# One core, local attention into a feed-forward layer: each engine's order written as a schedule of slots, weights loaded through other queues

## The chip, the core and the metric

One core of a Trainium2 chip runs the kernel. It has five engines that work side by side, each through its own list of instructions in order: TensorE (matmuls, into the accumulation memory PSUM), VectorE, ScalarE, GpSimd, and SyncE, which here only issues transfers (DMAs). An instruction waits on semaphores for what it needs, and everything behind it on its engine waits with it. The profile calls the engines PE, DVE, ACT, POOL and SP; PEld is TensorE's weight load. The metric is device time in microseconds (us).

## The reference

Attention over 4 batches, 8 heads, 768 positions and 64 values per head. A query sees its last 96 keys and the first 8 keys of the sequence, with a bias that grows with distance. The result, as 3072 tokens of 512 values, goes through a feed-forward layer of width 1024 with a gate h * softmax(h) and a layer norm without mean shift.

```python
    scores = scale * np.matmul(q, k.transpose(0, 1, 3, 2))
    is_global = pos[None, :] < int(n_global)
    is_local = (rel >= 0) & (rel < int(n_local))
    ...
    bias = -slopes[:, None, None] * dist[None, :, :]
    scores = np.where(keep, scores + bias, -1e9)
    a = np.exp(scores - max); a = a / (sum(a) + 1e-09)
    x = np.matmul(a, v)
    ...
    h = x @ w_in
    solu = h * softmax(h)
    ln = (solu - mu) / np.sqrt(var + 1e-06) * g_ln
    return ln @ w_out
```

(Lines of the reference, shortened.)

## The kernel before

The work is cut into 12 units of 256 queries, three in each batch (s = 0, 1, 2), and each unit's feed-forward into two tiles of 128 tokens, r0 and r1. For a unit the steps are: q and k are loaded, cast to 16 bits by GpSimd (L211) and turned on TensorE by eight matmuls each against a unit matrix (L227); VectorE copies them out of PSUM as qT and kT (L234, L240). Four groups of heads have scores (L262), an Exp on ScalarE (L267) and a product with a mask of bias and window on VectorE (L269). The eight global keys have small matmuls of their own (gs, L281; Exp L287; values pv, L294). Sums of the weights (lp, L307 and L315) go through Ln and Exp on ScalarE to 1/l (rl, L322); four transfers spread rl over the partitions as rlb (L326). Values (pa, L343, L351) times rlb give xT on VectorE (L358).

The feed-forward of a tile: ph = xT w_in, eight matmuls with 512 columns (L370); Exp on ScalarE (e, L377); the product un on VectorE (L380); Square on ScalarE (L386); five GpSimd instructions on a column of 128 that give the norm's factor rs (L391 to L398). Then eight transposes of un (lT, L406), a copy by VectorE (uT, L408), eight matmuls with gw (po, L411), and the scaling by rs, on VectorE for r0 (L419), on ScalarE for r1 (L421), into osb, which SyncE stores (L423).

gw is w_out times g_ln, less its mean over the rows: scaled on VectorE, averaged by eight matmuls (gbar, L458), and centred on VectorE (L461). The masks are 16 Exps on ScalarE (L203) of distances that VectorE works out from GpSimd's indices. All transfers are issued by SyncE, in one queue. w_in comes as 32-bit numbers and is cast on VectorE.

PSUM has three buffers of two banks ("big": scores, ph, pa) and two of one bank ("small": turned q and k, gs, pv, lp, lT, po).

The order is written by a weave: while the feed-forward of unit i is issued step by step (ff_in of a tile, then ff_out of the tile before), the attention of unit i + 2 is issued between its steps, two units ahead. From this order the framework's scheduler makes each engine's list, by its own estimates of when things are ready; it moves single matmuls past each other.

Of the kernel before, what the change touches and what calls it, by code (L numbers as in the profile page):

```python
# [16 lines left out]
P = 128  # L17
# [5 lines left out]
def kernel(  # L23
# [86 lines left out]
    def constants():  # L110
        c = held
        c["ident"] = ident = const.tile([P, P], FP16, name="ident")
# [5 lines left out]

# [15 lines left out]
        far = msb.tile([P, W0 + W1], FP32, name="far", tag="osb", bufs=2)
# [37 lines left out]
        for g in range(NPAIR):  # L172
            for m in range(2):
                nc.gpsimd.tensor_copy(
                    out=selV[:, g, m * NG : m * NG + NG].rearrange("p (r i) -> p r i", r=2),
                    in_=ident.rearrange("p (r i) -> p r i", r=2)[:, :, 0 : NG // 2],
                )
# [21 lines left out]

    def masks(kind):  # L200
        o, w = ((0, W0), (W0, W1))[kind]
        for h in range(H):
            nc.scalar.activation(out=held["mask"][:, h // 2, h % 2, o : o + w],  # L203
                                 in_=held["dist"][:, o : o + w],
                                 func=AF.Exp, scale=-slopes[h])


    def cast_qk(b, s):
        for name in "qk":
            t = attn.tile([P, 2, H, D], FP16, name=name + "16")  # L210
            nc.gpsimd.tensor_copy(  # L211
                out=t, in_=held.pop((name + "32", b, s)).rearrange("p h (r d) -> p r h d", r=2)
            )
            held[name + "16", b, s] = t
# [7 lines left out]
    def turn(b, s, name):  # L222
        src = held.pop((name + "16", b, s))
        pt_ = small([P, NPAIR, 2, P], FP16, "p" + name)
# [7 lines left out]
        if name == "q":  # L232
            qT = attn.tile([P, NPAIR, 2, QC], FP16, name="qT")
            nc.vector.tensor_copy(out=qT, in_=pt_)  # L234
            held["qT", b, s] = qT
            return
        if s == 0:
# [4 lines left out]
            in_=pt_.rearrange("p g r (j i) -> p (g r) j i", j=2),  # L242
        )
        if s == 0:
            z = held["kgz"][b % 2]
            for m in range(2):
                rr = slice(m * D, m * D + D)
                nc.gpsimd.tensor_copy(
                    out=z[rr, :, m * NG : m * NG + NG].rearrange("p g (r i) -> p g r i", r=2),
                    in_=kT[rr, 0, :, :, 0 : NG // 2],  # L250
                )

    def scores(b, s, g):
# [13 lines left out]
        nc.scalar.activation(out=pt[:, :, 0:w], in_=sc[:, :, 0:w], func=AF.Exp, scale=inv_sqrt_d)  # L267
        o = W0 if s else 0
# [6 lines left out]
    def global_scores(b, s):  # L275
# [3 lines left out]
        gs = small([P, 2, n], FP32, "gs")  # L279
# [6 lines left out]
        pg = attn.tile([P, 2, n], FP16, name="pg", bufs=3)  # L286
        nc.scalar.activation(out=pg, in_=gs, func=AF.Exp, scale=inv_sqrt_d, bias=held["gb"])  # L287
        held["pg", b, s] = pg

    def global_values(b):  # L290
        pv = small([P, HD], FP32, "pv")
        v0 = attn.tile([P, HD], FP16, name="v0", bufs=1)
        nc.gpsimd.tensor_copy(out=v0.rearrange("p (h d) -> p h d", d=D), in_=held["v16", b][:, :, 0])
        nc.tensor.matmul(out=pv, lhsT=held["selV"].rearrange("p g c -> p (g c)"), rhs=v0,  # L294
# [6 lines left out]
    def sums(b, s):  # L301
        i0 = gstart(s)
        lp = small([P, 2, QC], FP32, "lp")
# [14 lines left out]
        )  # L318
        ln = attn.tile([P, UQ], FP32, name="ln")
        nc.scalar.activation(out=ln, in_=lp.rearrange("p r i -> p (r i)"), func=AF.Ln)  # L320
        rl = attn.tile([P, UQ], FP32, name="rl")
        nc.scalar.activation(out=rl, in_=ln, func=AF.Exp, scale=-1.0)  # L322
        rlb = attn.tile([P, NPAIR, UQ], FP32, name="rlb", bufs=3)
# [7 lines left out]
        held["rlb", b, s] = rlb  # L331

    def values(b, s, gs):
        if gs[0] == 0:
            held["po", b, s] = big("pa").rearrange("p a f -> p (a f)").rearrange(
                "p (g r i) -> p g r i", g=NPAIR, r=2)
        po = held["po", b, s]
        i0 = gstart(s)
        for g in gs:
# [10 lines left out]
        for g in gs:  # L350
# [5 lines left out]
    def norm(b, s):  # L356
        xT = attn.tile([P, NPAIR, UQ], FP16, name="xT", bufs=3)
        nc.vector.tensor_tensor(  # L358
            out=xT, in0=held.pop(("po", b, s)).rearrange("p g r i -> p g (r i)"),
# [5 lines left out]
    def ff_in(b, s, r):  # L365
        xT = held["xT", b, s]
        ph = big("ph").rearrange("p a f -> p (a f)")
        for j in range(NCC):
            for fh in range(2):
                nc.tensor.matmul(  # L370
                    out=ph[:, ds(fh * 512, 512)], lhsT=xT[:, j, ts(r, P)],
# [3 lines left out]
        e = msb.tile([P, D_FF], FP16, name="e")  # L375
        s0 = msb.tile([P, 1], FP32, name="s0", bufs=6)
        nc.scalar.activation(out=e, in_=ph, func=AF.Exp, accum_out=s0)  # L377
        un = msb.tile([P, D_FF], FP16, name="un", bufs=4)
        s1 = msb.tile([P, 1], FP32, name="s1", bufs=6)
        nc.vector.scalar_tensor_tensor(  # L380
            out=un, in0=e, scalar=1.0, in1=ph,
            op0=ALU.mult, op1=ALU.mult, accum_out=s1,
        )
        sq = msb.tile([P, D_FF], FP16, name="sq", bufs=1)
        s2 = msb.tile([P, 1], FP32, name="s2", bufs=6)
        nc.scalar.activation(out=sq, in_=un, func=AF.Square, accum_out=s2)  # L386
# [13 lines left out]
        held["un", b, s, r], held["rs", b, s, r] = un, rs  # L400

    def ff_out(b, s, r):
        un, rs = held.pop(("un", b, s, r)), held.pop(("rs", b, s, r))
        lT = small([P, NFC, P], FP16, "lT")
        for u in range(NFC):
            nc.tensor.transpose(out=lT[:, u, :], in_=un[:, ts(u, P)], identity=held["ident"])  # L406
        uT = msb.tile([P, NFC, P], FP16, name="uT")
        nc.vector.tensor_copy(out=uT, in_=lT)  # L408
        po = small([P, D_MODEL], FP32, "po")
        for u in range(NFC):  # L410
# [3 lines left out]
            )  # L414
        if r == 0:
# [6 lines left out]
        if r == 1:  # L422
            nc.sync.dma_start(  # L423
                out=out[ds(b * S + s * UQ, UQ), :].rearrange("(p r) c -> p (r c)", r=2),
                in_=osb.rearrange("p r c -> p (r c)"),
# [3 lines left out]
    def w32(name):  # L429
        return stage.tile([P, 2 * D_MODEL], FP32, name=name, tag="w32", bufs=4)  # L430
# [147 lines left out]
```

## Time and profile before

| | us |
|---|---|
| median of 3 runs | 225.37 (224.7 to 228.64) |
| the profiled execution, its own time | 224.81 |
| its span, first to last instruction | 223.1 |
| mean granted TensorE clock | 0.965 |
| TensorE, VectorE, ScalarE, GpSimd busy | 174.8, 134.5, 120.3, 96.8 |

All that follows is read from the one profiled execution. A busy matmul in it includes its drain, which overlaps with the next one, so TensorE's busy time is more than its work; what it must do is better read from the distance between the starts of two pieces.

### The profile page before, as it was taken

How to read it: one execution, taken by the hardware profiler on the slowest of the kernel's cores; microseconds unless marked ns; L12 is line 12 of the kernel's file. 1: busy time of each engine (PE TensorE's matmuls, PEld its weight loads, DVE VectorE, ACT ScalarE, POOL GpSimd, SP SyncE). 2: the span in 40 equal slices, each digit the busy share in tenths (PEclk: the TensorE clock that was granted, in tenths of full speed). 3: DMA queues.
4: the chain of work that ended last, by engine and by line, in shares of the span. 5: the costliest groups of instructions: out<-in, count | busy, mean ns of one | idle time of the engine just before them, and what ended most of it. 6: DMA issues, size and time to landing. Idle time of an engine off the chain costs nothing.

```text
span 223.1 us, 4309 instructions
## 1 busy us (share of the span) xinstructions
PE 174.8 (78%) x1656; PEld 91.5 (41%) x1656; DVE 134.5 (60%) x215; ACT 120.3 (54%) x209; POOL 96.8 (43%) x196
## 2 busy tenths in 40 slices
PE   0247884679779799889799888996995995999962
PEld 0123542335435435535455345453353453454430
DVE  6784486865664844838765575767348357448550
ACT  2296530095663647583674845846454845746641
POOL 8934303353299253159366224954431231223340
PEclk9999999699996979999999999999699999999998
DMA  6999998999933999570799964973051213223022
GB/s 167 268 359 201 274 330 218 247 161 230 248 132 81 254 160 165 132 249 7 194 304 212 183 140 111 268 209 79 0 165 26 95 25 72 93 46 133 16 94 94
DMA packets 61188, 35.93 MB, mean 161 GB/s; under 512 B 27376, under 2 KB 58096, under 8 KB 61168
## 3 DMA queue, kind: packets, MB, share of 16 engines
q1 hardware_dynamic: 61168, 35.66, 69.9%
q8 instruction: 13, 0.21, 0.4%
q14 instruction: 7, 0.06, 0.1%
HBM read 23.07 MB, written 6.29 MB: 132 GB/s over the span
## 4 chain that ended last, share of the span: by engine, by line
PE 23%; DVE 7%; issue 7%; ACT 6%; DMA 5%; SPq 3%; POOL 2%; POOLq 0%; DVEq 0%
PE ph L370 8%; PE po L411 8%; DMA rlb<-rl 5%; SPq L326 3%; DVE un L380 2%; ACT e L377 2%; DVE uT L408 2%; PE lp L307 2%; ACT osb L421 1%; PE pa L343 1%; DVE pt L269 1%; PE lT L406 1%; DVE kT L240 1%; POOL w L397 1%; DVE xT L358 1%
## 5 line engine op out<-in xcount | busy, mean ns | idle before, releaser
L370 PE MATMUL ph<-w_in,xT 128*128 128x512 f16 x192 | 52.5, 406 | 7.6 <-DVE xT L358 5.4
L411 PE MATMUL po<-gw,uT 128*128 128x512 f16 x192 | 47.4, 388 | 4.2 <-DVE uT L408 3.0
L377 ACT ACTIVATE e<-ph 128x1024 f16<-128x1024 f32 x24 | 24.6, 1023 | 44.4 <-PE ph L370 44.2
L267 ACT ACTIVATE pt<-sc 128x896 f16<-128x896 f32 (+1 forms) x48 | 40.1, 858 | 5.4 <-PE sc L262 5.2
L269 DVE TENSOR_TENSOR pt<-pt,mask 128x896 f16<-128x896 f16 (+1 forms) x48 | 31.1, 660 | 18.3 <-ACT pt L267 17.9
L380 DVE SCALAR_TENSOR_TENSOR un<-e,ph 128x1024 f16<-128x1024 f16 x24 | 29.2, 1218 | 10.2 <-ACT e L377 10.0
L386 ACT ACTIVATE sq<-un 128x1024 f16<-128x1024 f16 x24 | 25.4, 1057 | 15.4 <-DVE un L380 15.3
L262 PE MATMUL sc<-qT,kT 64*128 64x224 f16 (+2 forms) x256 | 18.5, 246 | 17.7 <-ACT pt L267 6.6
L411 PEld LDWEIGHTS <-uT 128*128 128x128 f16 x192 | 18.3, 101 | 27.5 <-DVE uT L408 8.2
L370 PEld LDWEIGHTS <-xT 128*128 128x128 f16 x192 | 17.7, 102 | 26.5 <-issue 5.7
L391 POOL TENSOR_SCALAR w<-s 128x1 f32<-128x1 f32 x24 | 6.3, 261 | 48.7 <-ACT e L377 48.7
L393 POOL TENSOR_SCALAR w<-s,w 128x1 f32<-128x1 f32 x24 | 12.7, 531 | 26.4 <-DVE un L380 26.3
L419 DVE TENSOR_SCALAR osb<-po,rs 128x512 f32<-128x512 f32 x12 | 9.0, 750 | 21.3 <-POOL rs L398 13.4
L211 POOL CAST q<-q 128x1024 f16<-128x1024 f32 x12 | 13.1, 1091 | 18.3 <-DMA q<-in_q_dram 8.0
L262 PEld LDWEIGHTS <-kT 64*128 64x128 f16 x256 | 9.2, 98 | 27.1 <-issue 15.6
L408 DVE COPY uT<-lT 128x1024 f16<-128x1024 f16 x24 | 16.5, 686 | 5.9 <-PE lT L406 5.9
L343 PE MATMUL pa<-pt,v 128*64 128x128 f16 (+2 forms) x256 | 17.1, 256 | 0.5 <-ACT pt L267 0.5
L358 DVE TENSOR_TENSOR xT<-pa,rlb 128x1024 f16<-128x1024 f32 x12 | 14.6, 1218 | 2.4 <-DMA rlb<-rl 2.3
L211 POOL CAST k<-k 128x1024 f16<-128x1024 f32 x12 | 14.0, 1168 | 3.9 <-DMA k<-in_k_dram 3.3
L421 ACT ACTIVATE osb<-po,rs 128x512 f32<-128x512 f32 x12 | 8.2, 684 | 13.8 <-issue 6.9
L227 PE MATMUL pq<-ident,q 128*128 128x128 f16 x96 | 8.5, 233 | 9.0 <-POOL q L211 9.0
L406 PE MATMUL lT<-ident,un 128*128 128x128 f16 x192 | 15.1, 223 | 0.0
(68 smaller groups left out, 212.6 us busy)
## 6 DMA issues: line engine op xcount, KB each, us to landing
q<-in_q_dram SPq DMA_DIRECT2D x12, 512.0 KB, 4.9
k<-in_k_dram SPq DMA_DIRECT2D x12, 512.0 KB, 6.3
rlb<-rl SPq DMA_DIRECT2D x48, 128.0 KB, 2.8
out_dram<-osb SPq DMA_DIRECT2D x12, 512.0 KB, 2.7
v<-in_v_dram SPq DMA_DIRECT2D x6, 768.0 KB, 10.5
w_in<-in_moe_w_in_dram SPq DMA_DIRECT2D x4, 512.0 KB, 6.0
w_out<-in_moe_w_out_dram SPq DMA_DIRECT2D x4, 512.0 KB, 6.6
v<-in_v_dram SPq DMA_DIRECT2D x12, 128.0 KB, 5.1
```

The source lines that it names most:

```text
L211: nc.gpsimd.tensor_copy(out=t, in_=held.pop((name + "32", b, s)).rearrange("p h (r d) -> p r h d", r=2))
L262: nc.tensor.matmul(out=sc[:, m, o : o + e - a].rearrange("p (r i) -> p r i", r=2), lhsT=kT[r, j, g].rearrange("p r i -> p (r i)"), rhs=qT[ ...
L267: nc.scalar.activation(out=pt[:, :, 0:w], in_=sc[:, :, 0:w], func=AF.Exp, scale=inv_sqrt_d)
L269: nc.vector.tensor_tensor(out=pt[:, :, 0:w], in0=pt[:, :, 0:w], in1=held["mask"][:, g, :, o : o + w], op=ALU.mult)
L343: nc.tensor.matmul(out=po[m * D : m * D + D, g, :, a // 2 : e // 2], lhsT=held["v16", b][:, 2 * g + m, j], rhs=pt[:, m, o : o + e - a].rea ...
L370: nc.tensor.matmul(out=ph[:, ds(fh * 512, 512)], lhsT=xT[:, j, ts(r, P)], rhs=held["w_in"][:, j, ds(fh * 512, 512)], start=(j == 0), stop= ...
L377: nc.scalar.activation(out=e, in_=ph, func=AF.Exp, accum_out=s0)
L380: nc.vector.scalar_tensor_tensor(out=un, in0=e, scalar=1.0, in1=ph, op0=ALU.mult, op1=ALU.mult, accum_out=s1,)
L386: nc.scalar.activation(out=sq, in_=un, func=AF.Square, accum_out=s2)
L406: nc.tensor.transpose(out=lT[:, u, :], in_=un[:, ts(u, P)], identity=held["ident"])
L408: nc.vector.tensor_copy(out=uT, in_=lT)
L411: nc.tensor.matmul(out=po, lhsT=uT[:, u, :], rhs=held["gw"][:, u, :], start=(u == 0), stop=(u == NFC - 1),)
```

## The change

The scheduler is switched off. Each step is cut into its engine's part (scores, expo, keep; sums, invert, spread; ff_in, ff_exp, ff_mul, ff_square, ff_stats, ff_turn, ff_evac, ff_out, ff_scale, store), and a plan gives each part a slot and a time in it. The parts are sorted by slot x 13.2 + time, and this order alone stands on every engine; the numbers set an order, not a time. Slot i holds the feed-forward in of unit i, the output of unit i - 1 (one slot behind its input), the attention of unit i + 1, the turning of q and k of unit i + 2 and the load of q and k of unit i + 3. Slots -2 and -1 are the start.

The rest: q and k are turned into one big buffer; loads of w_in are issued by GpSimd and cast on the way, w_out and g_ln are issued by ScalarE; w_out is scaled on GpSimd; distances and masks are worked out in two halves, the second after the softmax of unit 0; q of unit 0 is cast on ScalarE; rlb and xT have two buffers, not three, un five, not four; the last unit is stored in two halves.

```diff
     def turn(b, s, name):
+        if name == "q":
+            held["turned"] = psum.tile([P, 2, NPAIR, 2, P], FP16, name="qk", tag="big", bufs=3)
         src = held.pop((name + "16", b, s))
-        pt_ = small([P, NPAIR, 2, P], FP16, "p" + name)
+        pt_ = held["turned"][:, "qk".index(name)]
...
     def load_w_in():
         held["w_in"] = const.tile([P, NCC, D_FF], FP16, name="w_in")
-        held["w_in32"] = [w32(f"w_in32_{j}") for j in range(NCC)]
-        for j in range(NCC):
-            nc.sync.dma_start(out=held["w_in32"][j], in_=moe_w_in[ts(j, P), :])
-
-    def cast_w_in():
-        for j in range(NCC):
-            nc.vector.tensor_copy(held["w_in"][:, j, :], held["w_in32"][j])
+        wv = moe_w_in.rearrange("(j p) f -> p j f", p=P)
+        for j in range(0, NCC, 2):
+            nc.gpsimd.dma_start(out=held["w_in"][:, j : j + 2], in_=wv[:, j : j + 2])
...
-        held["w_out32"] = []
-        for j in range(0, NFC, 2):
-            t = w32(f"w_out32_{j}").rearrange("p (j c) -> p j c", j=2)
-            nc.sync.dma_start(out=t, in_=wv[:, j : j + 2])
-            held["w_out32"] += [t[:, 0], t[:, 1]]
...
+        t = stage.tile([P, NFC, D_MODEL], FP32, name="w_out32", bufs=1)
+        for j in range(0, NFC, 4):
+            nc.scalar.dma_start(out=t[:, j : j + 4], in_=wv[:, j : j + 4])
+        held["w_out32"] = [t[:, j] for j in range(NFC)]
+
+    def scale_w_out(j):
+        if j == 0:
+            held["gw"] = const.tile([P, NFC, D_MODEL], FP16, name="gw")
+        nc.gpsimd.tensor_scalar(
+            out=held["gw"][:, j, :], in0=held["w_out32"][j], scalar1=held["g32"][:, j : j + 1],
+            scalar2=0.0, op0=ALU.mult, op1=ALU.add,
+        )
...
+    T = 13.2
+    plan = []
+
+    def at(slot, t, f, *args):
+        plan.append((slot * T + t, len(plan), f, args))
...
+        at(i - 2, 10.7, turn, b, s, "q")
+        at(i - 2, 11.3, turn, b, s, "k")
+        at(i - 2, 11.35, evac_q, b, s)
+        at(i - 2, 12.0, evac_k, b, s)
...
+        times = ((0, 4.6, 6.4, 7.65, 9.85), (1, 8.96, 11.1, 12.7, T + 0.5))
...
-    for i in range(N):
-        loads(i + 4)
-        prep(i + 3)
-        weave(attention(i + 2) if i + 2 < N else [], feed(i))
-    ff_out(*tiles[-1])
+    with tc.manual_schedule():
+        for _, _, f, args in sorted(plan, key=lambda x: x[:2]):
+            f(*args)
```

What this does to the lists. VectorE in the middle of the program, before: the copies of uT and xT stand between mask products, at places that differ from unit to unit.

```order
L380 SCALAR_TENSOR_TENSOR un,s_1233<-e,ph 128x1024
L408 COPY uT<-lT 128x1024
L269 TENSOR_TENSOR pt<-pt,mask 128x896 x3
L408 COPY uT<-lT 128x1024
L380 SCALAR_TENSOR_TENSOR un,s_1330<-e,ph 128x1024
L269 TENSOR_TENSOR pt<-pt,mask 128x896
L358 TENSOR_TENSOR xT<-pa,rlb 128x1024
L419 TENSOR_SCALAR osb<-po,rs 128x512
L234 COPY qT<-pq 128x1024
L240 COPY kT<-pk 128x8x2x64
L380 SCALAR_TENSOR_TENSOR un,s_1476<-e,ph 128x1024
L408 COPY uT<-lT 128x1024
```

VectorE in the same part, after: one pattern in every slot, here from un of r1 to the next.

```order
L414 SCALAR_TENSOR_TENSOR un,s_1266<-e,ph 128x1024
L447 COPY uT<-lT 128x1024
L385 TENSOR_TENSOR xT<-pa,rlb 128x1024
L290 TENSOR_TENSOR pt<-pt,mask 128x896
L465 TENSOR_SCALAR osb<-po,rs 128x512
L290 TENSOR_TENSOR pt<-pt,mask 128x896
L447 COPY uT<-lT 128x1024
L290 TENSOR_TENSOR pt<-pt,mask 128x896 x2
L414 SCALAR_TENSOR_TENSOR un,s_1397<-e,ph 128x1024
L248 COPY qT<-qk 128x1024
L255 COPY kT<-qk 128x8x2x64
L414 SCALAR_TENSOR_TENSOR un,s_1512<-e,ph 128x1024
```

The un of r1 stands behind qT and kT and directly ahead of uT of r0; xT comes ahead of all mask products of its slot.

SyncE at the start, before (q, k, v: the inputs; w_in, g, w_out: weights; rlb: the spread of 1/l):

```order
L86 DMA q_155<-in_q_dram 128x8x128
L86 DMA k_157<-in_k_dram 128x8x128
L104 DMA v_75<-in_v_dram 64x8x64 x8
L444 DMA g_167<-in_moe_g_ln_dram 128x8x1
L449 DMA w_out_0_169<-in_moe_w_out_dram 128x2x512
L449 DMA w_out_2_171<-in_moe_w_out_dram 128x2x512
L449 DMA w_out_4_173<-in_moe_w_out_dram 128x2x512
L449 DMA w_out_6_175<-in_moe_w_out_dram 128x2x512
L86 DMA q_177<-in_q_dram 128x8x128
L86 DMA k_179<-in_k_dram 128x8x128
L326 DMA rlb<-rl 128x1x256 x8
```

SyncE at the start, after:

```order
L86 DMA q_82<-in_q_dram 128x8x128
L86 DMA k_84<-in_k_dram 128x8x128
L86 DMA q_86<-in_q_dram 128x8x128
L86 DMA k_88<-in_k_dram 128x8x128
L356 DMA rlb<-rl 128x1x256 x4
L104 DMA v_77<-in_v_dram 64x8x64 x8
L86 DMA q_351<-in_q_dram 128x8x128
L86 DMA k_353<-in_k_dram 128x8x128
L356 DMA rlb<-rl 128x1x256 x4
```

The weights have left this list, the rlb of unit 0 stands directly behind q and k of unit 2, and the second part of v behind it.

SyncE in a slot that loads v, after (osb is the stored output):

```order
L356 DMA rlb<-rl 128x1x256 x4
L86 DMA q_1277<-in_q_dram 128x8x128
L86 DMA k_1279<-in_k_dram 128x8x128
L98 DMA v_1286<-in_v_dram 64x48x64 x2
L473 DMA out_dram<-osb 128x1024
L356 DMA rlb<-rl 128x1x256 x4
L86 DMA q_1523<-in_q_dram 128x8x128
```

The store and the rlb of the slot stand behind the two loads of v, as they did before.

## Rows read from the trace of the kernel before

**Rows 1.** The cores view, then the page's line of busy engines: us, share, instructions.

```profile
core 0: 223.1 us, clock 0.965
...
PE 174.8 (78%) x1656; PEld 91.5 (41%) x1656; DVE 134.5 (60%) x215; ACT 120.3 (54%) x209; POOL 96.8 (43%) x196
```

**Rows 2.** Tile view of osb: duration ns min/median/max, first and last start us.

```profile
L421 ACT ACTIVATE osb<-po,rs x12: 668/687/689, 62.3 to 218.9; 128x512 f32<-128x512 f32 x12
```

**Rows 3.** The chain that ended last, two steady stretches: start us, us, what.

```profile
125.73 0.22 PE gs L281 x4
...
126.11 1.83 PE ph L370 x8
127.95 0.30 PE sc L262 x6
...
128.59 0.57 PE lT L406 x8
...
133.30 0.49 PE lp L307 x21
133.79 0.21 PE lp L315
...
134.65 0.45 PE pq L227 x8
...
197.25 1.73 PE po L411 x8
198.97 0.32 PE pa L343 x6
199.29 0.33 PE pa L351 x2
```

**Rows 4.** Timeline of one tile: start us, us, engine, line, what, [idle before].

```profile
200.30 1.02 ACT L377 ACTIVATE e<-ph 128x1024 f16<-128x1024 f32 x1 [2.18 <-PE ph L370]
...
201.44 1.22 DVE L380 SCALAR_TENSOR_TENSOR un<-e,ph 128x1024 f16<-128x1024 f16 x1
...
202.71 1.06 ACT L386 ACTIVATE sq<-un 128x1024 f16<-128x1024 f16 x1 [1.29 <-DVE un L380]
```

**Rows 5.** Costliest groups by form: xcount | busy us, mean ns | idle before.

```profile
L358 DVE TENSOR_TENSOR xT<-pa,rlb 128x1024 f16<-128x1024 f32 x12 | 14.6, 1218 | 2.4 <-DMA rlb<-rl 2.3
...
L240 DVE COPY kT<-pk 128x1024 f16<-128x1024 f16 x12 | 8.3, 691 | 7.3 <-PE pk L227 7.3
...
L203 ACT ACTIVATE mask<-dist 128x448 f16<-128x448 f32 x8 | 3.9, 563 | 7.9 <-DVE dist L140 7.9
```

**Rows 6.** The chain that ended last, after one softmax: start us, us, what.

```profile
181.60 0.42 ACT rl L322
...
183.92 2.65 DMA rlb<-rl
```

**Rows 7.** Tile views of v (72:76, then whole) and rlb (116:122): landings, issues.

```profile
DMA to landing us min/median/max: 10.3/12.1/13.8
...
L104 SPq DMA_DIRECT2D v<-in_v_dram x12: 711/832/3418, 1.9 to 20.1; - x12
...
DMA to landing us min/median/max: 7.2/7.4/9.9
```

**Rows 8.** Timeline of the start: start us, us, engine, line, what.

```profile
23.17 0.42 ACT L322 ACTIVATE rl<-ln 128x256 f32<-128x256 f32 x1
...
28.60 7.89 SPq L326 DMA_DIRECT2D rlb<-rl  x8
...
35.54 4.04 DVE L461 SCALAR_TENSOR_TENSOR gw<-w_out,g,gbar 128x512 f16<-128x512 f32 x6 [2.47 <-PE gbar L458]
...
40.77 3.33 PE L370 MATMUL ph<-w_in,xT 128*128 128x512 f16 x8 [4.82 <-DVE xT L358]
```

**Rows 9.** Windows view, two stretches: us, busy by engine, TensorE clock, DMA share, GB/s.

```profile
24.00:37.00 13.00, 9.94 (x103) 5.55 (x101) 8.30 (x17) 4.62 (x7) 3.72 (x4) 1.00 1.04 306
40.70:44.00 3.30, 3.23 (x10) 1.20 (x11) 3.06 (x5) 0.00 (x0) 1.10 (x2) 0.55 1.29 224
```

More of the change, by code (lines that the diff above doesn't have):

```diff
@@ L198, in constants, with zeros @@
         c["neghalf"] = neghalf
+    def zeros():
+        held["kgz"] = []
+        for i in range(2):
+            z = const.tile([P, NPAIR, 32], FP16, name=f"kgz{i}")
+            nc.gpsimd.memset(z, 0.0)
+            held["kgz"].append(z)
     def masks(kind):
@@ L203, in masks, with cast_q @@
             nc.scalar.activation(out=held["mask"][:, h // 2, h % 2, o : o + w],
[L204 to L214, printed above, removed]
+                                 in_=held["dist", kind], func=AF.Exp, scale=-slopes[h])
+    def cast_q(b, s, name):
+        t = attn.tile([P, 2, H, D], FP16, name=name + "16")
+        src = held.pop((name + "32", b, s)).rearrange("p h (r d) -> p r h d", r=2)
+        if (b, s, name) == (0, 0, "q"):
+            nc.scalar.activation(out=t, in_=src, func=AF.Copy)
+        else:
+            nc.gpsimd.tensor_copy(out=t, in_=src)
+        held[name + "16", b, s] = t
     def cast_v(b, s):
@@ L330, in sums, with values @@
             )
[L331 to L337, printed above, removed]
+    def values(b, s):
+        po = held["pa", b, s] = big("pa").rearrange("p a f -> p (a f)").rearrange(
+            "p (g r i) -> p g r i", g=NPAIR, r=2)
         i0 = gstart(s)
-        for g in gs:
+        for g in range(NPAIR):
             pt = held["pt", b, s, g]
@@ L349, in values @@
                     )
-        for g in gs:
+        for g in range(NPAIR):
             nc.tensor.matmul(
@@ L421, in ff_out, with store @@
             nc.scalar.activation(out=osb[:, r], in_=po, func=AF.Copy, scale=rs)
[L422 to L425, printed above, removed]
-            )
-    def w32(name):
-        return stage.tile([P, 2 * D_MODEL], FP32, name=name, tag="w32", bufs=4)
+    def store(b, s, r=None):
+        rows = out[ds(b * S + s * UQ, UQ), :].rearrange("(p r) c -> p r c", r=2)
+        osb = held["osb", b, s]
+        sl = slice(0, 2) if r is None else slice(r, r + 1)
+        nc.sync.dma_start(out=rows[:, sl], in_=osb[:, sl])
@@ L498, in weave @@
-    def weave(one, two):
-        one, two = list(one), list(two)
-        done = 0
-        for i, step in enumerate(one):
-            step()
-            while done < len(two) and done * len(one) < (i + 1) * len(two):
-                two[done]()
-                done += 1
-        for step in two[done:]:
-            step()
-    tiles = [(b, s, r) for b, s in units for r in range(2)]
-    def feed(i):
-        for t in (2 * i, 2 * i + 1):
-            yield lambda t=t: ff_in(*tiles[t])
-            if t:
-                yield lambda t=t: ff_out(*tiles[t - 1])
@@ new lines @@
+    at(-2, -9, load_qk, *units[0])
+    at(-2, -8, load_v, 0, (0, 1))
+    at(-2, -7, load_qk, *units[1])
+    at(-2, -6, load_qk, *units[2])
+    at(-2, -4, key_offsets)
+    at(-2, -3.1, query_offsets, 0)
+    at(-2, -3, distances, 0)
+    at(-2, -2, zeros)
+    at(-2, 0.6, masks, 0)
+    at(-2, 0.7, load_w_out)
+    at(-2, 0.8, load_w_in)
+    at(-2, 0.9, query_offsets, 1)
+    at(-1, 0.26, constants)
+    at(-1, 6.7, distances, 1)
+    at(-1, 9.2, masks, 1)
+    at(-1, 10, load_v, 0, (2, 3, 4, 5))
```

294 lines of the change are left out of this document (159 added, 135 removed).

## The prediction

> **What bounds the kernel now.** I read the engines' shares first, then the tile view of the output buffer, the chain that ended last in two steady stretches, the timeline of the tail and of the start, and last the landings. TensorE is busy 78% of the span, VectorE and ScalarE 60% and 54% [rows 1], so no engine is full. The output buffer shows the rhythm: twelve ScalarE scalings from 62.3 to 218.9, one unit in (218.9 - 62.3) / 11 = 14.24 us [rows 2]. What TensorE must do in a unit comes from the chain, where pieces follow one another without overlap [rows 3]: feed-forward in 2 x 1.83, out 2 x 1.73, four groups of eight transposes at 0.45, four score groups at 0.30, global scores 0.22, sums 0.49 x 24/21 + 0.21 = 0.77, values 4 x 0.32 and two pairs of global values at 0.25 to 0.33: 12.8 to 13.0 us. So a unit loses some 1.3 us to orders that make TensorE wait, twelve times. The other loss is the start: the first feed-forward matmul runs at 40.77, after 4.82 us of waiting for xT, and its eight take 3.33 us where later ones take 1.83 [rows 3, 8], at a granted clock of 0.55, so near the lower level [rows 9].
>
> **The steady slot.** The change removes nothing that counts; it fixes the order. I walk one slot from the first matmul of the output of tile r0 (time 0), with the durations of [rows 3 to 5]. TensorE: output 1.83 (1.73 plus the 0.1 of a switch), transposes of r1 to 2.28, two score groups to 2.88, global scores to 3.10, feed-forward in r0 to 4.93, output r1 to 6.66, sums to 7.43, feed-forward in r1 to 9.26, q transposes to 9.71, k to 10.16. VectorE then copies qT from 9.26 + 0.59 = 9.85 (transposes to copy take 0.57 and 0.02) [rows 3], qT and kT take 0.69 each, to 11.23. Only behind them stands the product un of r1. It could start at 9.26 + 0.14 + 1.14 = 10.54 at the earliest, or 10.8 behind the Square of r0, which stands ahead on ScalarE (its start is 4.93 + 0.14 + 1.14 + 1.27 = 7.48 by the spacings of [rows 4], but ln and 1/l come first, so 8.3 to 9.6); so it starts at 11.23 and ends at 12.5. uT of r0, a copy as long as kT's, comes right behind (0.75 with its hops), and the next output starts at 13.25. TensorE meanwhile does values, transposes and two score groups, 10.16 + 1.8 + 0.45 + 0.6 = 13.0; it waits 0.25 us per slot. **So a slot takes 13.25 us**, where the engine's own work allows 12.9. In the slots whose attention is a first unit of a batch, there are fewer matmuls (scores -0.2, global scores -0.1, sums -0.25) and one for global values (+0.2): 12.9. Slots 1 to 9 are six of the one and three of the other: 118.2. Slot 10 has no transposes of q and k to wait for: un starts at 10.8 and the slot takes 12.85. Together 131.0, against 10 x 14.24 = 142.4.
>
> **What must be hidden for that.** The normalizer rlb: sums end at 7.43, ln and 1/l to 8.3, and from the end of 1/l to the last landing the chain shows 186.57 - 182.02 = 4.55 us (four issues 0.63 apart, then 2.65) [rows 6]: 12.9, that is 0.35 ahead of the next slot's zero. xT (1.22), a mask product (taken as long as a copy, 0.69) and the scaling of r0 (as ScalarE's, 0.7) stand behind each other on VectorE [rows 2, 5] and end at 2.7; the global scores need the scaling's buffer at 2.88. So rlb may come about 0.5 late before TensorE waits. **Twice it comes later than that.** In slots 4 and 7 SyncE issues q, k, then v, then the store, then the four rlb, in one queue. v needs the cast of its last user (GpSimd, about 0.75 in the slot). A v behind q and k lands 10.3 and 13.8 us after its issues [rows 7]; counted from q's issue (-2.5) that is 14.0, then store and rlb follow: about 16.7, or 3.4 in the next slot, and TensorE waits some 2.7 us. The bounds are 0 (transfers pass each other) and 4.8 (four rlb behind half a v landed 7.4 us after issue where 2.6 is usual) [rows 6, 7]. I take 2.7, twice: 5.4. In slot 1 the load is issued early enough, since slot 0 is long.
>
> The trace shows that queue as one line: an rlb issued behind v waits for it [rows 7]. The Trainium skill (Perfetto Trace Analysis, DMA Optimizations) advises splitting input and output between issuing engines; the change leaves loads, stores and rlb together on SyncE. By that advice a version with rlb on a queue of its own would be 5.4 us better than my sum.
>
> **The start.** Before, 1/l of unit 0 ends at 23.59 [rows 8]; eight of the sixteen masks (8 x 0.563) [rows 5] now come after it, so 19.1. xT of unit 0 then waited for two things: the eight rlb issues ran from 28.60 to 36.5, behind the weights and q and k of unit 2, and VectorE centred gw from 35.54 to 39.58 ahead of it [rows 8]. Now rlb of unit 0 stands behind q and k of units 1 and 2 alone, and xT ahead of the centring. If nothing else were moving it would land at 19.1 + 4.55 = 23.7. But all weights move at the same time, and the 16 engines were full before (their share is 1.04 from 24 to 37) [rows 9]. As one full queue, before, the last rlb landed at 36.5 + 2.65 = 39.1; eight issues of v (0.83 each) [rows 7] and the four rlb of unit 1 (0.63 each) now come after it: 39.1 - 6.6 - 2.5 = 30. I take 30, nearest to the row of a full queue; the ends are 23.7 and 39.1 - 2.5 = 36.6. From there: xT 1.22, then two score groups and global scores, which wait for the buffer that xT frees, 0.82: 32.0. Feed-forward in at the lower clock 3.33, sums 0.77, the mean of the weights like an output 1.83: 38.0. The centring of gw stays on VectorE, six took 4.04 [rows 8], so eight 5.4, ahead of qT and kT of unit 2: 43.4, copies 1.4, un 1.27, uT 0.75: **the first output matmul at 46.9**, which is zero of slot 1. Other edits of the start lie under this: the cast of q on ScalarE, the smaller mask chain and the two w_in loads issued by GpSimd with the cast inside the transfer (no row shows such a load; an issue on SyncE takes 0.7 to 3.4 [rows 7], so two of them 1 to 7 us on GpSimd) have 30 - 19.1 = 11 us of cover; w_in itself must land by 32. The eight scalings of w_out go to GpSimd, at most 1.34 each (twice that VectorE time), half of them after the second half has landed (30): 36 at the latest, when the mean wants them. The casts of w_in that leave VectorE saved nothing on the path.
>
> Before, one queue carried all loads, full, and rlb waited in it [rows 8, 9]. The Trainium skill (DMA: Bandwidth & Descriptors, Issuing engines are not separate DMA queues) says that DMAs of different issuing engines run on the same 16 engines and interleave, which saves only issue time. By that rule alone the start would gain nothing but order; it is the second rival below.
>
> **The tail.** From zero of slot 11: output 1.83, transposes 0.45, feed-forward in r0 and ScalarE's Exp at 4.25 (1.83 + 0.14), un 1.14 later, Square 1.27 later (6.66), Exp of r1 behind it at 7.9, un 9.05, end 10.3, uT 11.05, output to 13.0, scaling 0.7, uT of r1 0.75, output to 16.5, scaling by ScalarE. From that scaling's start to the span's end the tail of before takes 223.1 - 218.9 = 4.2 [rows 1, 2]: 20.7. TensorE waits three times there, so I add 1.0 for the lower clock: 21.7.
>
> **Sum.** 46.9 + 131.0 + 5.4 + 21.7 = 205.0 us of span. The profiled execution of before took 224.81 with a span of 223.1, so 1.7 more: **207 us**. The profiled time lies 0.56 under the median of the three runs (225.37), less than their spread; I make no correction.
>
> **Rivals.** *(a) All goes as walked: 207.* *(b) The start is as long as before:* weights on other queues take the transfer time from q, k and rlb, rlb of unit 0 lands at 36.6 and the first output comes 6.6 later: 214. For it: the full engines of [rows 9]; against: the order in the one queue, which made rlb wait for loads that nobody needed yet. *(c) No better rhythm:* the waits only move, and ten slots cost 142.4 as before: 207 + 11.4 = 218; with (b) as well 225, no change by this measurement. A fixed order has no other work to take up when one piece is late, which speaks for it; the walk, where TensorE is within 0.35 of its own work, against. *(d) The lower clock in each slot:* if TensorE's short waits drop the clock in every slot as the wait of 4.82 did, one feed-forward group in each costs 3.33 - 1.83 = 1.5 more: 207 + 15 = 222. Against it: the mean granted clock of before is 0.965 [rows 1], though it waits over 1 us in each unit. *(e) Slower than before:* in each slot the four rlb stand directly behind a store of 512 KB in one queue, issued 0.7 us ahead of them. If they cannot start until it has landed, rlb is late in ten slots, not two. The point from which this decides is the 0.5 us of slack; from there each 0.1 costs 1 us. The half of v that cost 4.8 has 768 KB; by size a store costs 4.8 x 512 / 768 = 3.2, so (3.2 - 0.5) x 10 = 27 on top: 234. For it: the rlb behind v [rows 7]. Against it: a store moves in few long rows, v in many short ones, and rlb's four issues take 2.5 us themselves, in which the store runs out.
>
> **How the numbers follow.** Chances: (a) with its own bounds 0.62; (b) 0.12; (c) alone 0.08, with (b) 0.04; (d) 0.06; (e) 0.06; the rest 0.02. Low end: 207 less the free start (30 - 23.7 = 6.3) and less the two late rlb (5.4), 196. High end: 219, which takes in (b) with v at its upper bound (2 x 2.1 more), and (c); it leaves out (d), (e), and (b) with (c). A measurement of this kernel can tell about 2% from no change, 4.5 us: faster means under 220.9. That holds for (a), (b), (c) and a third of (d): 0.84; within 2%, to 229.9, the rest of (d) and (b) with (c): 0.09; slower: 0.07.
>
> **What would show it.** Scalings of the output by ScalarE 13.1 us apart on the mean, not 14.2; the first output matmul near 47 with xT of unit 0 released by rlb at about 30; VectorE's un of r1 right behind kT in each slot; two waits of about 3 us on the way to global scores, after the loads of v for the third and fourth batch. The prediction is wrong if rlb lands late in every slot, if GpSimd's weight loads land after 32 us, or if granted clocks under 1 stand in the steady slots.

## The result, and the profile after

The changed kernel took 217.36 us (median of four runs, 215.56 to 219.1) against 225.27 for the kernel before (the median of four; the 225.37 given above is of three): a ratio of 0.963, 95% interval 0.955 to 0.971, so 3.7% faster. The forecast was 207, range 196 to 219. In the ratios of e1 to e4 below only two runs of the kernel before count, because the others ran in a slower state. The profiled execution of the changed kernel (called *after* from here on) is the longest of the four (219.1 us). Its cores view and line of busy engines answer to [rows 1]:

```profile
core 0: 217.4 us, clock 0.958
...
PE 165.9 (76%) x1656; PEld 92.9 (43%) x1656; DVE 123.6 (57%) x208; ACT 120.3 (55%) x210; POOL 95.5 (44%) x205
```

The tile view of the output buffer (duration ns min/median/max, first and last start us) answers to [rows 2]:

```profile
L467 ACT ACTIVATE osb<-po,rs x12: 681/687/688, 57.0 to 213.5; 128x512 f32<-128x512 f32 x12
...
who waited for it (us, times):
  PE gs L302: 10.4, 5
```

The mean rhythm is (213.5 - 57.0) / 11 = 14.23 us, where it was 14.24 [rows 2]. So the slots as a whole won nothing: the span is 5.7 us shorter, and 5.3 of that were won before the first of these scalings, which came at 62.3 and now comes at 57.0. But the mean hides two kinds of slot. The windows view, cut at the first output matmul of slots 1, 2, 4, 5, 7, 8 and 9 and of the slot behind (columns: stretch, length, busy us by engine, TensorE's clock, DMA share, GB/s):

```profile
48.66:63.41 14.75, 14.10 (x141) 7.89 (x142) 9.10 (x14) 9.46 (x17) 5.16 (x12) 0.88 1.04 169
63.41:77.56 14.15, 12.17 (x126) 6.89 (x127) 9.18 (x15) 8.67 (x17) 9.03 (x16) 1.00 0.56 157
91.26:104.67 13.41, 12.51 (x141) 7.36 (x142) 8.88 (x14) 9.48 (x17) 6.71 (x15) 1.00 1.27 198
104.67:125.47 20.80, 14.61 (x126) 7.51 (x127) 9.17 (x15) 8.78 (x17) 7.99 (x16) 0.84 0.53 153
...
151.90:170.83 18.93, 13.64 (x127) 7.26 (x127) 9.22 (x16) 8.78 (x17) 8.00 (x16) 0.91 0.55 165
170.83:183.96 13.13, 12.57 (x146) 7.40 (x146) 9.05 (x15) 9.48 (x17) 5.06 (x14) 1.00 0.27 81
...
112.30:114.00 1.70, 1.67 (x8) 0.69 (x8) 1.70 (x4) 0.29 (x1) 0.00 (x0) 0.50 0.01 4
```

A quiet slot takes 13.1 to 13.7 us at full clock. Slots 5 and 8, the ones behind the loads of v, take 20.80 and 18.93, at a granted clock of 0.84 and 0.91 of 2.4 GHz; part of each ran at the lower level, 1.2 GHz (the last line is such a part of slot 5, at 0.50). In e5 and e11 below, which are alike there, they take 18.46 and 19.03, and 20.49 and 18.69. What happens there, from the timeline of slots 4, 5 and 8 (the last four lines from the view of TensorE alone):

```profile
91.92 5.23 SPq L98 DMA_DIRECT2D v<-in_v_dram  x2
...
99.01 2.98 SPq L473 DMA_DIRECT2D out_dram<-osb  x1
...
102.11 2.57 SPq L356 DMA_DIRECT2D rlb<-rl  x4
...
109.96 1.22 DVE L385 TENSOR_TENSOR xT<-pa,rlb 128x1024 f16<-128x1024 f32 x1 [5.35 <-DMA rlb<-rl]
...
111.53 0.74 DVE L465 TENSOR_SCALAR osb<-po,rs 128x512 f32<-128x512 f32 x1
...
112.33 0.22 PE L302 MATMUL gs<-qT,kgz 128*32 128x32 f16 x4 [4.91 <-DVE osb L465]
112.48 3.59 PE L397 MATMUL ph<-w_in,xT 128*128 128x512 f16 x8
115.87 2.66 PE L453 MATMUL po<-gw,uT 128*128 128x512 f16 x8
...
158.65 0.22 PE L302 MATMUL gs<-qT,kgz 128*32 128x32 f16 x4 [3.99 <-DVE osb L465]
158.80 3.36 PE L397 MATMUL ph<-w_in,xT 128*128 128x512 f16 x8
```

This is the chain that the prediction described: xT waits for rlb, the scaling stands behind xT on VectorE, and the global scores wait for the scaling's buffer. Behind the two waits, groups of eight matmuls that take 1.90 at full clock take 3.59, 2.66 and 3.36. The landings in the tile views of v (window 91:93) and of rlb (102:105, then 86:89, one slot earlier) answer to [rows 6, 7]; min/median/max in us:

```profile
DMA to landing us min/median/max: 9.3/11.3/13.3
```

```profile
DMA to landing us min/median/max: 5.8/6.2/6.5
...
DMA to landing us min/median/max: 2.6/3.3/3.5
```

The second half of v, issued at 92.6, lands 13.3 us later, at 105.9, and rlb behind it by 109.9, 5.2 us past zero of slot 5. The DMA view of 94:105 shows what the engines do meanwhile: every slice is full, at 286 to 290 GB/s while q and k move and then mostly 150 to 163 for v.

```profile
DMA  9999999999999999999999999999999999999999
GB/s 290 290 286 286 270 248 179 179 161 153 163 158 152 155 155 153 152 158 150 152 156 158 181 193 189 171 160 151 158 154 155 155 153 155 155 152 162 210 187 324
DMA packets 6834, 2.03 MB, mean 184 GB/s; under 512 B 6192, under 2 KB 6803, under 8 KB 6833
```

The 1.57 MB of v at 154 GB/s make 10.2 us; k ahead of it has landed by 96.1, so v by 106.3, an estimate with the rate of this same stretch: the landing fits the bytes ahead of it. The start, from the timeline, answers to [rows 8]:

```profile
20.37 0.42 ACT L349 ACTIVATE rl<-ln 128x256 f32<-128x256 f32 x1
...
32.00 1.23 DVE L385 TENSOR_TENSOR xT<-pa,rlb 128x1024 f16<-128x1024 f32 x1 [3.68 <-DMA rlb<-rl]
...
33.28 3.59 PE L397 MATMUL ph<-w_in,xT 128*128 128x512 f16 x8 [4.29 <-DVE xT L385]
...
37.86 2.41 PE L502 MATMUL gbar<-gw,meanw 128*128 128x512 f16 x8
...
40.31 5.36 DVE L507 SCALAR_TENSOR_TENSOR gw<-w_out,g,gbar 128x512 f16<-128x512 f32 x8 [1.02 <-PE gbar L502]
```

The first feed-forward matmul comes at 33.28, 7.5 us earlier than before, and the first output matmul at 48.66.

### The profile page after: what moved, and what is told of

Same layout as the page of the kernel before. It is cut to its first block, busy times and chain, and to the rows that moved or that the text cites. A ratio compares the mean times of both kernels' runs of the same rounds, so it can differ in the third digit from the quotient of the medians.

```text
span 217.4 us, 4299 instructions
## 1 busy us (share of the span) xinstructions
PE 165.9 (76%) x1656; PEld 92.9 (43%) x1656; DVE 123.6 (57%) x208; ACT 120.3 (55%) x210; POOL 95.5 (44%) x205
## 5 line engine op out<-in xcount | busy, mean ns | idle before, releaser
L453 PE MATMUL po<-gw,uT 128*128 128x512 f16 x192 | 48.9, 401 | 7.4 <-DVE uT L447 7.4
L397 PE MATMUL ph<-w_in,xT 128*128 128x512 f16 x192 | 50.3, 409 | 4.3 <-DVE xT L385 4.3
L284 ACT ACTIVATE pt<-sc 128x896 f16<-128x896 f32 (+1 forms) x48 | 38.4, 857 | 11.1 <-PE sc L275 11.1
L453 PEld LDWEIGHTS <-uT 128*128 128x128 f16 x192 | 18.6, 102 | 32.2 <-DVE uT L447 10.0
L290 DVE TENSOR_TENSOR pt<-pt,mask 128x896 f16<-128x896 f16 (+1 forms) x48 | 29.6, 635 | 2.9 <-ACT pt L284 2.7
L428 POOL TENSOR_SCALAR w<-s 128x1 f32<-128x1 f32 x24 | 6.2, 260 | 48.9 <-ACT e L409 48.7
L248 DVE COPY qT<-qk 128x1024 f16<-128x1024 f16 x12 | 8.3, 691 | 28.5 <-PE qk L239 28.5
L275 PE MATMUL sc<-qT,kT 64*128 64x128 f16 (+2 forms) x256 | 16.1, 245 | 9.8 <-DVE un L414 5.2
L430 POOL TENSOR_SCALAR w<-s,w 128x1 f32<-128x1 f32 x24 | 9.5, 395 | 18.3 <-DVE un L414 17.5
L432 POOL TENSOR_SCALAR w<-s,w 128x1 f32<-128x1 f32 x24 | 7.2, 302 | 22.0 <-ACT sq L422 21.2
L223 POOL CAST k<-k 128x1024 f16<-128x1024 f32 x12 | 12.5, 1040 | 8.7 <-DMA k<-in_k_dram 8.7
L230 POOL CAST v<-v 128x1024 f16<-128x1024 f32 x12 | 12.5, 1039 | 8.4 <-DMA v<-in_v_dram 6.7
L275 PEld LDWEIGHTS <-kT 64*128 64x128 f16 x256 | 9.2, 99 | 14.6 <-issue 8.3
L434 POOL TENSOR_TENSOR w<-w,neghalf 128x1 f32<-128x1 f32 x24 | 14.2, 591 | 2.0
```

Source lines behind the costliest of these rows:

```text
L275: nc.tensor.matmul(out=sc[:, m, o : o + e - a].rearrange("p (r i) -> p r i", r=2), lhsT=kT[r, j, g].rearrange("p r i -> p (r i)"), rhs=qT[ ...
L284: nc.scalar.activation(out=pt[:, :, 0:w], in_=held.pop(("sc", b, s, g))[:, :, 0:w], func=AF.Exp, scale=inv_sqrt_d)
L290: nc.vector.tensor_tensor(out=pt[:, :, 0:w], in0=pt[:, :, 0:w], in1=held["mask"][:, g, :, o : o + w], op=ALU.mult)
L397: nc.tensor.matmul(out=ph[:, ds(fh * 512, 512)], lhsT=held["xT", b, s][:, j, ts(r, P)], rhs=held["w_in"][:, j, ds(fh * 512, 512)], start=( ...
L434: nc.gpsimd.tensor_tensor(out=w4, in0=w3, in1=held["neghalf"], op=ALU.pow)
L453: nc.tensor.matmul(out=po, lhsT=uT[:, u, :], rhs=held["gw"][:, u, :], start=(u == 0), stop=(u == NFC - 1),)
```

## The experiments

Two theories were held against each other on the late rlb. *Queue:* it waits for what stands ahead of it in SyncE's one queue. *Shared engines:* it waits for all bytes issued earlier, whoever issued them. A third question was the clock. Each kernel was timed beside the kernel before on the same chip (ratios are to that; after has 0.963).

**e4_no_v.** The v loads of batches 1 to 3 are left out, so those batches use the v of batch 0.

```diff
-                at(i - 2, 0.35, load_v, b)
+                pass
...
-        nc.gpsimd.tensor_copy(out=held["v16", b][:, :, sl], in_=held["v32", b][:, :, sl])
+        nc.gpsimd.tensor_copy(out=held["v16", b][:, :, sl], in_=held["v32", 0][:, :, sl])
```

> Kernel after without the v loads of batches 1 to 3: the casts read v of batch 0 again, so these batches are computed with the wrong v. Both theories: no v ahead of rlb, slots 5 and 8 take about 13.2, 203 to 206; this is the most that moving v can give. If it stays above 212, v is not the cause of the long slots.

205.42 us, ratio 0.915 (0.897 to 0.933). Slots 5 and 8 took 13.81 and 13.52. The loads of v are the cause of the long slots, 12 us in all.

**e2_v_thirds.** The same bytes in three slots:

```diff
-                at(i - 2, 0.35, load_v, b)
+                at(i - 2, 0.35, load_v, b, (0, 1))
+                at(i - 1, 0.35, load_v, b, (2, 3))
+                at(i, 0.35, load_v, b, (4, 5))
```

> Kernel after, with each v load split into thirds that are issued by SyncE in three successive slots, 0.5 MB each. Queue theory and bandwidth theory alike: 1.5 MB held rlb up by 5.2 and 4.3 us past the slot's end (in quiet slots it lands about in time), so a third holds it up by some 0 to 1.5 in each of nine slots instead of two: 206 to 215. If only the size of the lump counts it comes to the low end, if every byte ahead of rlb counts to the high one.

202.72 us, ratio 0.905 (0.893 to 0.918): better than expected, and no worse than without v. Its windows of slots 4, 5 and 8:

```profile
87.71:101.29 13.58, 12.51 (x142) 7.35 (x142) 8.88 (x14) 9.47 (x17) 6.29 (x15) 1.00 0.88 203
101.29:114.91 13.62, 12.17 (x127) 6.90 (x127) 9.42 (x15) 8.66 (x17) 8.51 (x16) 1.00 0.82 190
141.44:154.95 13.51, 12.17 (x127) 6.90 (x127) 9.32 (x16) 8.67 (x17) 9.05 (x16) 1.00 0.86 203
```

By that rate a third takes 10.2 / 3 = 3.4 us of the engines; in slot 4 it has landed by 96.5, when 1/l is ready (96.4). So the bytes fit into the slots; only the lump did not.

**e1_v_scalar_queue, e3_rlb_scalar_queue, e9_two_rlb_scalar.** Three ways to part v and rlb into two queues: v from ScalarE (at 1.0 in the slot), every rlb from ScalarE, or rlb from ScalarE in slots 4 and 7 alone.

```diff
     def load_v(b, js=None):
+        eng = nc.scalar if b else nc.sync
...
-                nc.sync.dma_start(
+                eng.dma_start(
...
-                at(i - 2, 0.35, load_v, b)
+                at(i - 2, 1.0, load_v, b)
```

```diff
     def spread(b, s):
...
-            nc.sync.dma_start(
+            nc.scalar.dma_start(
```

```diff
     def spread(b, s):
...
+        eng = nc.scalar if (b, s) in ((1, 2), (2, 2)) else nc.sync
...
-            nc.sync.dma_start(
+            eng.dma_start(
```

> Kernel after, with the three later v loads issued by ScalarE instead of SyncE. In the profile of after slots 5 and 8 take 20.80 and 18.93 us where the others take about 13.2, so 13.2 us hang on those two. Queue theory (rlb waits because it stands behind v and a store in SyncE's one queue): rlb lands in time, slots 5 and 8 take 13.2 to 14, the time falls from 217.4 by 11 to 13, to 204 to 206. Bandwidth theory (v of 1.5 MB fills the 16 engines for some 14 us whoever issues it): rlb still lands late, 18 us after the slot's zero, and the time falls by at most 4, to 213 to 217.

> Kernel after, with all rlb issued by ScalarE behind 1/l; v, q, k and the stores stay on SyncE. Queue theory: rlb waits for nothing in any slot, slots 5 and 8 take 13.2 to 14, and the start gains too (rlb of unit 0 landed 11 us after 1/l), less up to 0.5 per slot for four issues of 0.6 us each on ScalarE ahead of Exp: 202 to 209. Bandwidth theory: rlb shares the engines with v and the store and comes as late as before: 213 to 219.

> Kernel after, with rlb issued by ScalarE in slots 4 and 7 alone, the two in which v is loaded; v, the store and everything else stay on SyncE. Queue theory (rlb waits only for what stands ahead of it in SyncE's queue): rlb lands some 3 us after its issue, before v has landed, slots 5 and 8 take 13 to 15 and the time is 204 to 208. Shared-engine theory (transfers go in the order of their issue, whichever engine issued them): rlb lands with or after v and the store, 6 to 9 us after its issue, slots 5 and 8 stay at 19 to 22 and the time at 216 to 222.

e1 took 221.60 us (ratio 0.987, 0.963 to 1.012), e3 248.79 (1.110, 1.095 to 1.124), e9 213.48 (0.941, 0.935 to 0.947). None came where either theory put its time. In e1 the two issues of v held ScalarE, and its next Exp came after 5.39 us of that (timeline):

```profile
91.09 5.21 ACTq L99 DMA_DIRECT2D v<-in_v_dram  x2
...
96.34 3.35 ACT L285 ACTIVATE pt<-sc 128x896 f16<-128x896 f32 x4 [5.39 <-issue]
```

In after the same issues held SyncE as long (5.23 above), which has nothing else to do. So e1 swaps the wait for another (slots 4 and 7 take 20.66 and 20.62, slots 5 and 8 13.65 and 13.63) and can't tell the theories apart. In e3 the four issues took 2.5 to 4.4 us of ScalarE in each slot, ahead of Square and of Exp of r1, which lead to the next slot's first output: I had put 0.5 on that, and slots took some 17. Even in slot 2, which has no v, rlb took 4.8 to 8.0 us there to land, beside q and k, which SyncE issued at the same time. e9 does tell the theories apart, by the landing and not by its time (timeline, then the landings in the tile views of v and of rlb, then the windows view of slots 4 and 5):

```profile
98.72 2.62 ACTq L357 DMA_DIRECT2D rlb<-rl  x4
...
101.39 1.06 ACT L423 ACTIVATE sq<-un 128x1024 f16<-128x1024 f16 x1 [2.70 <-issue]
...
109.13 1.22 DVE L386 TENSOR_TENSOR xT<-pa,rlb 128x1024 f16<-128x1024 f32 x1 [3.73 <-DMA rlb<-rl]
```

```profile
DMA to landing us min/median/max: 9.4/11.5/13.5
...
DMA to landing us min/median/max: 7.3/7.7/8.3
```

```profile
90.09:105.46 15.37, 12.51 (x142) 7.36 (x142) 8.97 (x14) 9.59 (x17) 5.93 (x13) 1.00 1.26 207
105.46:122.21 16.75, 14.03 (x126) 7.39 (x127) 9.17 (x16) 8.88 (x17) 8.87 (x18) 0.90 0.57 161
```

On a queue with nothing ahead of it, rlb landed 7.3 to 8.3 us after its issue, at 106.6 to 109.0, all of it after the second half of v (104.9). In a quiet slot it takes 2.6 to 3.5. That is the shared engines, not the queue. Nor did rlb take anything from v, whose second half landed 13.5 us after its issue, in after 13.3. Counted from zero of slot 4, rlb was issued at 8.6 and had landed at 18.9; in after, where it stands behind a store whose issue is held up, at 10.9 and 18.6. So the earlier issue won nothing, and the 4 us that e9 won on after are not explained by it. Slots 4 and 5 take 32.12 together, 2.1 less than in after, but 32.29 in e5, which is alike with after there.

**e5_w_out_sync, e11_w_in_sync, e8_before_weights.** The weights part of the change: w_out and g_ln back on SyncE, w_in back on SyncE with casts on VectorE, and the kernel before with the weights part alone.

```diff
     def load_w_out():
...
-            nc.scalar.dma_start(out=t[:, j : j + 4], in_=wv[:, j : j + 4])
+            nc.sync.dma_start(out=t[:, j : j + 4], in_=wv[:, j : j + 4])
```

```diff
-            nc.gpsimd.dma_start(out=held["w_in"][:, j : j + 2], in_=wv[:, j : j + 2])
...
+            nc.sync.dma_start(out=t, in_=moe_w_in[ts(j, P), :])
...
+    at(0, 3.4, cast_w_in)
```

```diff
-            nc.sync.dma_start(out=held["w_in32"][j], in_=moe_w_in[ts(j, P), :])
...
+            nc.gpsimd.dma_start(out=held["w_in"][:, j : j + 2], in_=wv[:, j : j + 2])
...
-            nc.sync.dma_start(out=t, in_=wv[:, j : j + 2])
...
+            nc.scalar.dma_start(out=t[:, j : j + 4], in_=wv[:, j : j + 4])
...
-    cast_w_in()
```

> Kernel after, with w_out (2 MB) issued by SyncE again, behind q and k of units 0 to 2 and ahead of rlb of unit 0; w_in stays on GpSimd. If the start is set by the bytes that the 16 engines must move ahead of rlb of unit 0, whoever issues them, nothing changes: rlb lands at 31 to 33 as in after, 216 to 219. If it is set by what stands ahead of rlb in its own queue, rlb lands some 8 us later and the time is 223 to 227.

> Kernel after, with w_in loaded as before: four loads of 512 KB by SyncE, behind q and k of unit 2 and ahead of rlb of unit 0, and four casts on VectorE, just ahead of xT of unit 0. Bytes alike whoever issues them: rlb of unit 0 lands at 31 to 33 as in after, the casts cost 0 to 2 us on the way to the first feed-forward matmul: 216 to 220. Queue theory: 2 MB more ahead of rlb in its queue, 8 us: 223 to 227.

> Kernel before with the weights part of the change alone: w_in by two casting loads of GpSimd (no casts on VectorE), w_out by two loads of ScalarE; the planner's order stays. If rlb of unit 0 was late because it stood behind the weights in one queue, the first feed-forward matmul comes at 33 to 36 instead of 40.77, and 217 to 221. If the start is set by all bytes alike or by other work, 223 to 228.

e5: 218.57 us (0.964, 0.957 to 0.971); e11: 218.08 (0.953, 0.943 to 0.964). Both as the shared engines want it: with 2 MB more ahead of it in its queue, rlb of unit 0 landed at 31.9 and 30.5, in after at 31.9. e8 missed: 234.17 (1.029, 1.022 to 1.036), slower than before, with the first feed-forward matmul at 47.90 instead of 40.77. ScalarE has nothing ahead of its weight loads in that kernel and issues them at 1.3 us, so k of unit 0 lands 8.9 us after its issue instead of 5.8; and VectorE stands 12.2 us at the scaling of the weights, ahead of kT. How the loss splits between the two wasn't tried. So the queue part of the change is worth nothing that these runs show; what was gained came with the rest, the fixed order and the work that moved with it (masks in halves, w_out scaled on GpSimd), and no run parts those.

**e7_filler, e12_tail_filler.** Work put into a wait of TensorE: 40 repeated score matmuls in slots 5 and 8 of after, and ten unread matmuls in the tail of e10 below.

```diff
+            if g == 1 and i in (6, 9):
+                at(i - 1, 1.0, filler, b, s, g, 40)
```

```diff
+    at(N - 1, 8.25, tail_filler, 10)
```

> Kernel after, with 40 score matmuls of group 1 repeated (same result) where TensorE waits 4.9 us in slots 5 and 8, some 3.9 us of work inside the wait. Clock theory: the feed-forward and output matmuls behind the wait run at the higher level, 1.9 instead of 3.59 and 3.36 us, and po of r1 at 1.9 instead of 2.66: 4 us in all, 212.5 to 214.5. If the lower clock has nothing to do with the wait, or the filler only takes the wait's place, 217 to 220.

> Kernel e10_store_after, with ten matmuls whose result nobody reads in the tail's wait for uT (2.63 us in e6), so that TensorE does not stand still there. Clock theory: the next eight output matmuls take 1.90 instead of 3.27, so 1.0 to 1.4 us less than e10. Otherwise equal to e10 or up to 0.5 more.

e7: 213.68 us (0.939, 0.933 to 0.945), 3.7 under after and 4.9 under e5, which ran beside it and behaves like after. rlb was as late as before (xT waited 5.12), yet the groups behind the wait ran at 1.90 us and the clock stood at 1.00 in both slots (timeline, then the windows view of slot 5):

```profile
101.63 3.99 PE L285 MATMUL sc<-qT,kT 64*128 64x224 f16 x40
...
109.52 0.20 PE L312 MATMUL gs<-qT,kgz 128*32 128x32 f16 x4 [1.21 <-DVE osb L475]
109.66 1.90 PE L407 MATMUL ph<-w_in,xT 128*128 128x512 f16 x8
...
105.56:120.23 14.67, 12.17 (x128) 6.90 (x127) 9.23 (x16) 7.72 (x14) 5.91 (x12) 1.00 0.55 157
```

The filler stands ahead of the output group of r0, so it lengthened slot 4 to 16.71 and cut slot 5 to 14.67; the gain is the clock, not the wait. In these slots a wait that stops TensorE is paid twice: once as such, once in the lower clock behind it.

e12: 199.72 (0.881, 0.874 to 0.887) against 200.95 for e10; the two intervals overlap. The tail's output group went from 2.89 to 1.90 us, but the filler need not be the cause. Behind the same wait without a filler, this group took 2.79 to 3.55 in after, e1, e4, e5, e6, e10 and e11, and 1.90 in e2, e7 and e9 (timelines of after and of e2):

```profile
206.77 3.27 PE L453 MATMUL po<-gw,uT 128*128 128x512 f16 x8 [2.63 <-DVE uT L447]
...
190.87 1.90 PE L453 MATMUL po<-gw,uT 128*128 128x512 f16 x8 [2.63 <-DVE uT L447]
```

**e6_thirds_mean_early, e10_store_after.** On top of e2: the mean and the centring of the weights earlier; then the store behind rlb.

```diff
-    at(0, 8.95, mean_w_out)
-    at(0, 9.0, centre_w_out)
+    at(0, 4.5, mean_w_out)
+    at(0, 6.1, centre_w_out, range(4))
+    at(0, 6.5, centre_w_out, range(4, NFC))
```

```diff
-            at(i + 1, 8.9, store, b, s)
+            at(i + 1, 9.2, store, b, s)
```

> Kernel e2_v_thirds (202.7 us), with the mean of the weights moved ahead of the first feed-forward matmul, where TensorE waits for xT, and the centring done in two halves on VectorE, ahead of un of r0 and behind it. First output matmul at about 44 instead of 46.7, and 200 us (199 to 201.5). If something else sets the start (rlb of unit 1, the buffers of the small tiles), 202 to 204.

> Kernel e6_thirds_mean_early (200.1 us), with the store of each unit issued behind the four rlb of the slot instead of ahead of them. If the store's 512 KB ahead of rlb is what is left of rlb's lateness (slots at 13.4 to 13.9 where 13.1 is the least), most slots take 13.1 to 13.3: 197 to 199. If rlb is late for other reasons, or not late, 199.5 to 201.

e6: 200.09 us (0.880, 0.874 to 0.887), first output matmul at 44.34, as expected. e10: 200.95 (0.884, 0.877 to 0.892), no gain: slots 1 to 9 still took 13.1 to 14.1, so the store ahead of rlb is not what is left. e6 and e12 are the best versions, 12% under before.

## Why the prediction was right and wrong

Sign and range held; the size did not. That the range held is in part luck: its upper end was made of rivals (b) and (c), and what came was neither as described. Step by step, predicted and measured span in the profiled execution (slots 5 and 8 were 2 x 12.9 + 5.4 = 31.2, the other eight 118.2 + 12.85 - 25.8 = 105.25):

| Part | predicted | measured | difference |
|---|---|---|---|
| first output matmul | 46.9 | 48.66 | +1.8 |
| slots 1 to 10 without 5 and 8 | 105.25 | 107.78 | +2.5 |
| slots 5 and 8, late rlb included | 31.2 | 39.73 | +8.5 |
| tail | 21.7 | 21.2 | -0.5 |
| span | 205.0 | 217.4 | +12.4 |

**The steady slot was right.** 13.25 was walked; slots 6, 7 and 9 took 13.30, 13.13 and 13.13, slots 3 and 4 13.70 and 13.41, slot 10 12.2 (12.85). The short slots were not right. Slots 2, 5 and 8, walked at 12.9, take 13.68, 13.62 and 13.51 in e2, where rlb is in time. In after their matmul of the global values waits 0.3 us for a buffer that ScalarE's scaling frees, which the walk left out; the rest stays open. Rival (d) is out: the clock holds in quiet slots. Rival (c) has the measured number (218), which is chance. Its reason, that a fixed order has no other work to take up when one piece is late, is what happened in two slots; but its rhythm of 14.24 in every slot did not come about.

**The step that failed is "Twice it comes later than that ... I take 2.7, twice: 5.4".** The place, the slots and the chain were right, the price too small by more than half. Slots 5 and 8 took 8.5 more than forecast, in three parts. *The wait, 3.5:* the waits ahead of the global scores were 4.91 and 3.99, together 8.9. v landed 14.6 us after zero of slot 4, near the 14.0 that I let it, although q was issued at -1.5 and not at -2.5; but the store and rlb behind it took another 4.0, where I had put 2.7. So rlb was done at 18.6, not 16.7. *The clock, 3.9:* I left out the lower clock behind these waits, although I had charged it at the start. Feed-forward in took 3.59 and 3.36 instead of 1.90, and the output of r1 2.66 instead of 1.89 (e7 gives 3.7 to 4.9 back). *The short slot, 1.1:* as said above. In e5 and e11 the two slots took 37.49 and 39.18 together, where after has 39.73, so the miss is 6.3 to 8.5. The upper bound of 4.8 fell because it looked only at the time from rlb's issue to its landing [rows 6, 7]: here the issue came late as well, 2.3 us behind 1/l (102.11 and 99.80).

**The reason given for it was also wrong.** I wrote of "one queue", and that a version with rlb on a queue of its own would be 5.4 us better. I drew that from advice of the Trainium skill, Perfetto Trace Analysis, section DMA Optimizations, on splitting inputs from outputs; rlb is neither, and no row showed it. e9 is that version for the two slots, e3 for all: rlb came after v all the same. The page that I had set against it, the Trainium skill, DMA: Bandwidth & Descriptors, section Issuing engines are not separate DMA queues, says that transfers of different issuers run on the same engines; e5, e9 and e11 agree. Where it says that such a move saves the issuer's time, e1 and e3 show the other side: the time goes to the engine that issues instead.

**The start** was 1.8 late: rlb landed at 31.9 (30), the mean took 2.41 (1.83; 1.89 in e1, e2, e5, e7 and e11), and the rest came as walked. In e1, e2 and e7, whose lists up to there differ at most in v of the second batch, the first output came at 46.21, 46.66 and 46.89, so the 1.8 is within what executions differ by. Rival (b) did not happen. **Slots 1 and 2** took 14.75 and 14.15. In slot 1 the first output group ran at the lower clock (3.16 instead of 1.90), after TensorE had waited 2.15 for kT, which VectorE copies behind the centring; in e6 and e10, which centre earlier, it took 1.90, but in e12, which does so too, 3.59. In slot 2 xT waited 1.11 for rlb. The v of the second batch, which I had called early enough, is not the reason: without it, in e4, the slot took 14.18 and xT waited 1.15. **Rival (e)** is out: the quiet slots, with the store directly ahead of rlb, took 13.1 to 13.7, and e10 moved the store and gained nothing.

## What to carry to other kernels

Price a transfer by all bytes issued ahead of it on any queue and by their rate, not by its queue, and spread a lump over the slots before moving it to another issuer. To a wait of 3 to 5 us that stops TensorE add the lower clock behind it (1.5 to 2.5 us here), or put idle work into the wait. Here an issue cost its engine 0.6 us, and 3.0 to 4.5 behind a v that was still moving, so issue from an engine that nobody waits for.

## What the runs showed of the hardware

v moved at some 154 GB/s with all engines full, q and k at 286 to 290; 6192 of the 6834 packets of that stretch are under 512 bytes, which may be why, but no run changed their size. The second of two issues of v took 4.5 us on SyncE and on ScalarE alike, against 0.6 for the first. In after, e5 and e11 each of the six waits of TensorE in slots 5 and 8, 3.31 to 5.00 us long, was followed by the low clock; in e7, where 40 small matmuls left waits of 1.21 and 0.98, it did not fall. Behind the tail's wait of 2.63 it fell in seven profiles and not in three. The granted clock of a profile does not always show it: the first feed-forward group of after took 3.59 in a stretch given as 1.00, as long as the one in slot 5 at 0.50. The first output matmul came anywhere from 46.2 to 48.7 us in six kernels whose start is the same but for v of the second batch (after, e1, e2, e4, e7, e9); why stays open.
